# A Fourier-mixing and two-FFN kernel on one core: its arithmetic on GpSimd moved to VectorE and ScalarE

## The chip, the core and the metric

The kernel runs on one core of a Trainium2 chip. The engines are named as the profile names them: PE is TensorE (PEld its weight loads), DVE is VectorE, ACT is ScalarE, POOL is GpSimd, SP is the engine that only issues DMAs. Each engine runs its own instructions in the order in which they stand in the program and waits for the others by semaphores. The metric is the time of one execution on the device in microseconds (us), as the median of several runs.

## The reference

```python
X = np.fft.rfft(x, axis=1)                      # x: 4 x 3072 x 256
Yr = Xr @ w_r - Xi @ w_i + b_r
Yi = Xr @ w_i + Xi @ w_r + b_i
Y  = shrink(Yr, 0.01) + 1j * shrink(Yi, 0.01)   # sign(v) * max(|v| - 0.01, 0)
y  = np.fft.irfft(Y, n=3072, axis=1)
xk = mu_k * y + (1 - mu_k) * y_prev             # y_prev: one position earlier
xr = mu_r * y + (1 - mu_r) * y_prev
k  = np.maximum(xk @ w_k, 0.0)                  # w_k: 256 x 1024
v  = k * k @ w_v                                # w_v: 1024 x 256
x  = sigmoid(xr @ w_rr) * v
h  = x @ w_in                                   # w_in: 256 x 2048
g  = h * np.clip(h + 3, 0, 6) / 6
out = g @ w_out                                 # w_out: 2048 x 256
```

[...]

## The kernel before

Every matmul is done in three passes on a high and a low part of each operand (`three`: high by high, low by high, high by low). So each operand is split first: ACT copies it rounded to its high part, and a subtraction (source minus high part) gives the low part. `split` (lines 145 to 148) does this and is told which engine subtracts, DVE or POOL.

The program has two halves. The first half, up to about 1062 us, does the Fourier mixing of four batches and the first FFN; the second half does the second FFN and has no arithmetic on POOL.

For each batch the mixing has three parts. `s1` reads chunks of x (tiles `a`, split into `ah` and `al`) and writes a first transform through DRAM. `mid` runs over 12 blocks j: `s2` (a transform into PSUM, split into `Xh` and `Xl`), `mix` (24 matmuls with w_r and w_i, then the shrink on DVE: `yf`, `ym`, `yf`), and `ia` (the first part of the inverse, from `yh` and `yl`, with the table tile `tt`, three buffers, loaded from DRAM by DMAs on POOL's queue). `ib` reads chunks again (`a`, `ah`, `al`) and ends on DVE with `ysb`, which frees its PSUM tile. A block of `mid` is 42 matmuls.

The first FFN works on 24 tiles of 512 tokens. `prep` makes a tile's two inputs (`xf` on ACT and DVE, then `kh` on ACT and `kl`); `u_r` and four units `u_k` with their `u_v` follow, 12 matmuls each for `pr`, `pk` and `acc`, so 108 for a tile. After each `pk` ACT makes `g` and its square `gh`, DVE multiplies `g` by itself (L549) and subtracts (`gl`, L550), and `acc` uses them two units later. From the second batch on, the mixing of the next batch is interleaved with FFN units.

`Weights.decode` (lines 184 to 209) turns 512 columns of a 64-bit weight into high and low parts, in four steps between which other work of the program is recorded: (1) three operations on DVE on the exponent word (extract, clamp, subtract and scale: L195, L196, L197), (2) three more on DVE (sign and exponent L199, mantissa L200, sum L201), (3) a product on POOL (L203), (4) `split` with its subtraction on POOL. There are 25 such jobs: 9 while the first batch is mixed, 16 (w_in, w_out) between about 800 and 1062 us, while the last tiles of the first FFN run.

On POOL in the first half stand: the subtraction of every second chunk (`al`, 88 of 176 together with 24 of 48 in `mid`), of every second `yl` (24 of 48), one half of every `kl` (48, the other half on DVE), of every decoded or plain weight (27), of one `xl`, the 25 products of the decode, and the DMAs of the tables.

The names are those of the profile: `al<-a,ah` is the instruction that writes a tile `al` from `a` and `ah`.

Of the kernel before, what the change touches and what calls it, by code (L numbers as in the profile page):

```python
# [9 lines left out]
F32 = mybir.dt.float32  # L10
# [4 lines left out]
ALU = mybir.AluOpType  # L15
# [88 lines left out]
def fourier_mix_ffn_kernel(  # L104
# [37 lines left out]
    def ptile(name):  # L142
        return ps.tile([128, 1024], F32, tag="h", name=name)

    def split(src, h, l, eng):

        nc.scalar.activation(h, src, AF.Copy)  # L147
        eng.tensor_sub(l, src, h.bitcast(F32))  # L148

    def three(o, pairs, first=True, last=True, **kw):  # L150

# [7 lines left out]
    class Weights:  # L159
# [24 lines left out]
        def decode(self, staged, k, q, c, m):  # L184
            w, t = staged
            yield
            hi, lo = self.hi[:, k : k + q, c : c + m], self.lo[:, k : k + q, c : c + m]
            if self.wide:
                w = w.rearrange("p k (n s) -> p k n s", s=2)
                low, high = w[:, :, :, 0], w[:, :, :, 1]  # L190
                a = t[:, 0].rearrange("p (k n) -> p k n", k=q)
                f = t[:, 1].rearrange("p (k n) -> p k n", k=q)
                ai, au = a.bitcast(I32), a.bitcast(U32)
                ts, stt = nc.vector.tensor_scalar, nc.vector.scalar_tensor_tensor
                ts(au, high, 20, 0x7FF, op0=ALU.logical_shift_right, op1=ALU.bitwise_and)  # L195
                ts(ai, ai, 916, 1170, op0=ALU.max, op1=ALU.min)  # L196
                ts(ai, ai, 916.0, 2.0**23, op0=ALU.subtract, op1=ALU.mult)  # L197
                yield
                stt(au, high, 0x80000000, au, op0=ALU.bitwise_and, op1=ALU.bitwise_or)  # L199
                ts(high, high, 0xFFFFF, 0x100000, op0=ALU.bitwise_and, op1=ALU.bitwise_or)  # L200
                stt(f, low, 2.0**-32, high, op0=ALU.mult, op1=ALU.add)  # L201
                yield
                nc.gpsimd.tensor_mul(f, f, a)  # L203
            else:
                f = w
                yield
                yield
            yield
            split(f, hi, lo, nc.gpsimd)

    def decoder(jobs, stage):

# [14 lines left out]
    with tc.manual_schedule(engines=order):  # L227
# [6 lines left out]
        mus = cst.tile([128, 2, 2], F32, name="mus")  # L234
        omu = cst.tile([128, 2, 2], F32, name="omu")
        half = cst.tile([128, 1], F32, name="half")
        bias = fp.tile([128, 3, D], F32, name="bias")
        tex = fp.tile([128, 2, 64], F32R, name="tex")

# [17 lines left out]
        def split_chunks(upto):  # L257
            while head["split"] < min(upto, head["load"]):
                n = head["split"]
                a, p = live[n]  # L260
                h = fp.tile([128, 2, D], F32R, tag="ah", bufs=4, name="ah")
                l = fp.tile([128, 2, D], F32R, tag="al", bufs=4, name="al")
                split(a, h[:p], l[:p], nc.gpsimd if n % 2 else nc.vector)
                live[n] = (h[:p], l[:p])
                head["split"] += 1

# [44 lines left out]
        def mid(b):  # L311
# [6 lines left out]
            def s2(j):  # L318
                ((h, l),) = take(1)
                t = tt[b, j]  # L320
                p = ptile("s2")
                for g in range(2):
                    for dt in range(2):
                        d = slice(128 * dt, 128 * dt + 128)
                        hl = (h[:, g, d], l[:, g, d])
                        if j or g:
                            c = 512 * g + 192 * dt
                            three(p[:, c : c + 192], [(hl, (t[:, g, 0:192], t[:, g, 192:384]))])
                        else:
                            c = 256 * dt  # L330
                            three(p[:, c : c + 64], [(hl, (t[:, g, 0:64], t[:, g, 192:256]))])
                            three(p[:, c + 64 : c + 128], [(hl, (tex[:, 0], tex[:, 1]))])
                            three(p[:, c + 128 : c + 256], [(hl, (t[:, g, 64:192], t[:, g, 256:384]))])
                xh = fp.tile([128, 896], F32R, tag="Xh", bufs=2, name="Xh")
                xl = fp.tile([128, 896], F32R, tag="Xl", bufs=2, name="Xl")
                if j == 0:
                    split(p[:, 0:896], xh, xl, nc.vector)
                else:
                    two = lambda v: v.rearrange("p (g f) -> p g f", g=2)
                    split(two(p)[:, :, 0:384], two(xh[:, 0:768]), two(xl[:, 0:768]), nc.vector)  # L340
                xx[j] = (xh, xl)

            def mix(j):
# [19 lines left out]

            def split_y(j):
                y, *yy[j] = yy[j]
                split(y, *yy[j], nc.gpsimd if j % 2 else nc.vector)

            def ia(j):
                yh, yl = yy.pop(j)
# [94 lines left out]
        load_chunks(5)  # L464
        nc.vector.memset(zero, 0.0)
        nc.vector.memset(half, 0.5)

        def vectors():
            for i, v in enumerate((b_r, b_i)):
# [18 lines left out]
        def prep(i):  # L488

            if i:  # L490
                y = yt.pop(i)
                before, now = [(0, TOK, y)], [(0, TOK, y[:, :, N1:])]
            else:

                y1, y2 = ysb.pop(1), ysb.pop(2)
                before = [(0, 352, y1[:, :, 32:]), (352, TOK, y2)]
                now = [(0, 256, y1[:, :, 128:]), (256, TOK, y2)]
            for w in (1, 0):
                xf = kb.tile([128, 2, TOK], F32, tag="xf", bufs=1, name="xf")
                for a in range(2):  # L500
                    for lo, hi, y in before:
                        nc.scalar.activation(xf[:, a, lo:hi], y[:, a, 0 : hi - lo], AF.Copy, scale=omu[:, w, a : a + 1])
                yield
                for a in range(2):
                    for lo, hi, y in now:
                        o = xf[:, a, lo:hi]
                        nc.vector.scalar_tensor_tensor(  # L507
                            o, y[:, a, 0 : hi - lo], mus[:, w, a : a + 1], o, op0=ALU.mult, op1=ALU.add
                        )
                yield  # L510
                h = kb.tile([128, 2, TOK], F32R, tag="kh", bufs=3, name="kh")
                l = kb.tile([128, 2, TOK], F32R, tag="kl", bufs=3, name="kl")
                nc.scalar.activation(h, xf, AF.Copy)  # L513
                nc.gpsimd.tensor_sub(l[:, 0], xf[:, 0], h[:, 0].bitcast(F32))  # L514
                nc.vector.tensor_sub(l[:, 1], xf[:, 1], h[:, 1].bitcast(F32))  # L515
                xs[i, w] = h, l
                yield

# [65 lines left out]
        def split_2(i):  # L584
            h = kb.tile([128, 2, TOK], F32R, tag="kh", bufs=3, name="xh2")
            l = kb.tile([128, 2, TOK], F32R, tag="kl", bufs=3, name="xl2")
            split(xt[i], h, l, nc.gpsimd)
            xt[i] = (h, l)

        def u_i(i, j):  # L590
# [10 lines left out]
            l = kb.tile([128, 1024], F32R, tag="gl", bufs=3, name="gl2")  # L601
            nc.scalar.activation(g, p, AF.Relu, bias=half, scale=1.0 / 6.0)
            nc.vector.scalar_tensor_tensor(g, g, 1.0, p, op0=ALU.min, op1=ALU.mult)
            split(g, h, l, nc.vector)
            hg[i, j] = (h, l)


# [375 lines left out]
```

## Time and profile before

| | |
|---|---|
| median of 3 runs | 2106.92 us (2104.93 to 2109.38) |
| the profiled execution's own time | 2105.2 us |
| span of its trace | 2103.4 us |
| PE busy, share of the span | 2017.2 us, 96% |
| DVE busy | 1579.2 us, 75% |
| ACT busy | 1290.6 us, 61% |
| POOL busy | 363.9 us, 17% |

Busy time is the time in which an engine worked on an instruction; an instruction that is held up in its middle counts as busy all the while. PE's matmuls are pipelined and overlap in the records, so a busy PE need not be at its peak; the number of matmuls in a stretch tells more. The granted clock (PEclk) is 1.00 where PE had 2.4 GHz throughout a stretch and 0.50 where it had 1.2 GHz.

### The profile page before, as it was taken

How to read it: one execution, taken by the hardware profiler on the slowest of the kernel's cores; microseconds unless marked ns; L12 is line 12 of the kernel's file. 1: busy time of each engine (PE TensorE's matmuls, PEld its weight loads, DVE VectorE, ACT ScalarE, POOL GpSimd, SP SyncE). 2: the span in 40 equal slices, each digit the busy share in tenths (PEclk: the TensorE clock that was granted, in tenths of full speed). 3: DMA queues.
4: the chain of work that ended last, by engine and by line, in shares of the span. 5: the costliest groups of instructions: out<-in, count | busy, mean ns of one | idle time of the engine just before them, and what ended most of it. 6: DMA issues, size and time to landing. Idle time of an engine off the chain costs nothing.

```text
span 2103.4 us, 34043 instructions
## 1 busy us (share of the span) xinstructions
PE 2017.2 (96%) x13928; PEld 1870.1 (89%) x13928; DVE 1579.2 (75%) x1858; ACT 1290.6 (61%) x1867; POOL 363.9 (17%) x276
## 2 busy tenths in 40 slices
PE   6878999999899999989998999999999999999999
PEld 4867997899789988768788999999999999999999
DVE  2988667667666677989978778777777777777775
ACT  5456447555664465545546677767776777667765
POOL 4455223222332132333310000000000000000000
PEclk7978999999999999999999999999999999999999
DMA  8765446543663242212101010100010011001100
GB/s 268 232 190 169 126 117 197 183 118 113 198 189 115 83 157 93 83 64 91 56 21 31 21 31 21 31 21 28 24 31 21 23 30 31 21 21 31 31 11 21
DMA packets 106991, 175.88 MB, mean 84 GB/s; under 512 B 12945, under 2 KB 63314, under 8 KB 106834
## 3 DMA queue, kind: packets, MB, share of 16 engines
q1 hardware_dynamic: 96034, 141.76, 21.8%
q0 software_dynamic: 10480, 31.67, 5.5%
q8 instruction: 109, 1.79, 0.4%
q14 instruction: 48, 0.39, 0.1%
q10 hardware_dynamic: 320, 0.26, 0.0%
HBM read 110.35 MB, written 63.31 MB: 83 GB/s over the span
## 4 chain that ended last, share of the span: by engine, by line
PE 79%; DVE 12%; ACT 3%; issue 2%; DMA 2%; POOL 1%; SPq 0%; ACTq 0%; DVEq 0%
PE oacc L773 25%; PE rq L773 15%; PE acc L156 9%; PE pk L156 7%; PE cc L773 6%; PE mix L156 5%; PE s L156 4%; PE pr L156 2%; DVE g L549 2%; DVE xf L507 2%; DVE gl L550 1%; PE ia L156 1%; PE ib L419 1%; PE ib L418 1%; DVE kl L515 1%
## 5 line engine op out<-in xcount | busy, mean ns | idle before, releaser
L773 PE MATMUL oacc<-wo_hi,gl 128*128 128x256 f32 x1536 | 432.9, 282 | 0.3 <-DVE gl L747 0.3
L773 PE MATMUL oacc<-wo_hi,gh 128*128 128x256 f32 x1536 | 432.0, 281 | 0.0
L773 PE MATMUL oacc<-wo_lo,gh 128*128 128x256 f32 x1536 | 429.9, 280 | 0.0
L773 PEld LDWEIGHTS oacc<-wo_hi,gh 128*128 128x128 f32 x1536 | 290.1, 189 | 0.2
L773 PEld LDWEIGHTS oacc<-wo_hi,gl 128*128 128x128 f32 x1536 | 289.3, 188 | 0.7 <-DVE gl L747 0.5
L773 PEld LDWEIGHTS oacc<-wo_lo,gh 128*128 128x128 f32 x1536 | 289.8, 189 | 0.0
L729 DVE TENSOR_TENSOR c<-rq,s 128x512 f32<-128x512 f32 x184 | 127.2, 691 | 184.8 <-ACT s L725 184.8
L742 DVE SCALAR_TENSOR_TENSOR g<-g,c 128x1024 f32<-128x1024 f32 x184 | 225.4, 1225 | 42.7 <-ACT g L741 37.9
L773 PE MATMUL rq<-th,sw 128*128 128x256 f32 x1104 | 221.0, 282 | 7.3 <-issue 7.3
L747 DVE TENSOR_TENSOR gl<-g,gh 128x1024 fp32r<-128x1024 f32 x184 | 223.6, 1215 | 1.2 <-ACT gh L746 1.2
L746 ACT ACTIVATE gh<-g 128x1024 fp32r<-128x1024 f32 x184 | 195.3, 1061 | 45.0 <-DVE g L742 45.0
L741 ACT ACTIVATE g<-c,half 128x1024 f32<-128x1024 f32 x184 | 210.7, 1145 | 2.2 <-DVE c L730 1.4
L709 ACT ACTIVATE s<-rq 128x512 f32<-128x512 f32 x184 | 110.2, 599 | 131.2 <-PE rq L773 129.0
L544 ACT ACTIVATE g<-pk 128x1024 f32<-128x1024 f32 x96 | 97.8, 1019 | 150.8 <-PE pk L156 150.6
L773 PEld LDWEIGHTS rq<-th,sw 128*128 128x128 f32 x1104 | 169.6, 189 | 7.4 <-issue 7.4
L156 PE MATMUL acc<-gl,wv_hi 128*128 128x512 f32 x384 | 152.8, 398 | 7.9 <-DVE gl L550 7.9
L148 POOL TENSOR_TENSOR al<-a,ah 96x512 fp32r<-96x512 f32 (+1 forms) x88 | 124.1, 1410 | 209.2 <-ACT ah L147 199.6
L773 PE MATMUL rq<-tl,sw 128*128 128x256 f32 x552 | 154.5, 280 | 2.7 <-DVE tl L676 2.7
L156 PE MATMUL pk<-kh,wk_hi 128*128 128x512 f32 x384 | 152.1, 396 | 2.8 <-ACT kh L513 2.5
L156 PE MATMUL acc<-gh,wv_hi 128*128 128x512 f32 x384 | 152.5, 397 | 0.0
L156 PE MATMUL pk<-kl,wk_hi 128*128 128x512 f32 x384 | 151.4, 394 | 1.2 <-POOL kl L514 1.2
L156 PE MATMUL acc<-gh,wv_lo 128*128 128x512 f32 x384 | 151.2, 394 | 0.0
(151 smaller groups left out, 5291.7 us busy)
## 6 DMA issues: line engine op xcount, KB each, us to landing
tt<-in_tab_dram POOLq DMA_DIRECT2D x40, 640.0 KB, 5.0
yt<-sc_y SPq DMA_DIRECT2D x23, 608.0 KB, 4.0
a<-in_x_dram SPq DMA_DIRECT2D x64, 192.0 KB, 3.3
sc_a<-s1sb SPq DMA_DIRECT2D x32, 384.0 KB, 3.7
a<-sc_a SPq DMA_DIRECT2D x48, 256.0 KB, 3.4
sc_b<-iasb SPq DMA_DIRECT2D x48, 256.0 KB, 4.9
a<-sc_b SPq DMA_DIRECT2D x64, 192.0 KB, 2.8
sc_y<-ysb SPq DMA_DIRECT2D x32, 384.0 KB, 2.8
```

The source lines that it names most:

```text
L148: eng.tensor_sub(l, src, h.bitcast(F32))
L156: nc.tensor.matmul(o, a, c, start=first and i == 0, stop=last and i == n - 1, **kw)
L507: nc.vector.scalar_tensor_tensor(o, y[:, a, 0 : hi - lo], mus[:, w, a : a + 1], o, op0=ALU.mult, op1=ALU.add)
L544: nc.scalar.activation(g, p, AF.Relu)
L549: nc.vector.tensor_mul(g, g, g)
L709: nc.scalar.activation(s[:, 1:3].rearrange("p a n -> p (a n)"), rq, AF.Copy)
L729: nc.vector.tensor_add(c[:, 1::2], two(rq), s[:, 0:2])
L741: nc.scalar.activation(g, c, AF.Relu, bias=half, scale=1.0 / 6.0)
L742: nc.vector.scalar_tensor_tensor(g, g, 1.0, c, op0=ALU.min, op1=ALU.mult)
L746: lambda: nc.scalar.activation(h, g, AF.Copy),
L747: lambda: nc.vector.tensor_sub(l, g, h.bitcast(F32)),
L773: return lambda: nc.tensor.matmul(o, lhs, rhs, start=start, stop=stop, skip_group_check=True)
```

## The change

All of POOL's arithmetic goes elsewhere. `split` loses its engine argument and always subtracts on DVE; `kl` is one subtraction of twice the width on DVE; the decode's product is on DVE. In the decode's first step the clamp and the scaling (two operations on DVE) become two ACT operations with Relu: the first gives max(1170 - a, 0), the second max(254 - that, 0) times 2 to the 23rd, which is the same clamp to 916..1170 less 916. They take their constants from a new tile `top`, set by two small memsets. POOL keeps the DMAs of the tables.

```diff
-    def split(src, h, l, eng):
+    def split(src, h, l):
         nc.scalar.activation(h, src, AF.Copy)
-        eng.tensor_sub(l, src, h.bitcast(F32))
+        nc.vector.tensor_sub(l, src, h.bitcast(F32))
...
                 ts(au, high, 20, 0x7FF, op0=ALU.logical_shift_right, op1=ALU.bitwise_and)
-                ts(ai, ai, 916, 1170, op0=ALU.max, op1=ALU.min)
-                ts(ai, ai, 916.0, 2.0**23, op0=ALU.subtract, op1=ALU.mult)
+                nc.scalar.activation(f, ai, AF.Relu, bias=top[:, 0], scale=-1.0)
+                nc.scalar.activation(ai, f, AF.Relu, bias=top[:, 1], scale=-(2.0**23))
                 yield
                 stt(au, high, 0x80000000, au, op0=ALU.bitwise_and, op1=ALU.bitwise_or)
...
-                nc.gpsimd.tensor_mul(f, f, a)
+                nc.vector.tensor_mul(f, f, a)
...
-            split(f, hi, lo, nc.gpsimd)
+            split(f, hi, lo)
...
-                split(a, h[:p], l[:p], nc.gpsimd if n % 2 else nc.vector)
+                split(a, h[:p], l[:p])
...
-                split(y, *yy[j], nc.gpsimd if j % 2 else nc.vector)
+                split(y, *yy[j])
...
+        nc.vector.memset(top[:, 0], 1170.0)
+        nc.vector.memset(top[:, 1], 254 * 2.0**23)
...
-                nc.gpsimd.tensor_sub(l[:, 0], xf[:, 0], h[:, 0].bitcast(F32))
-                nc.vector.tensor_sub(l[:, 1], xf[:, 1], h[:, 1].bitcast(F32))
+                nc.vector.tensor_sub(l, xf, h.bitcast(F32))
...
-            split(xt[i], h, l, nc.gpsimd)
+            split(xt[i], h, l)
```

PE's instructions stand in the same order before and after. Three places where other engines' rows change:

DVE in `mid` of the first batch, one pair of blocks with one decode job, before (`Xl`, `yl`, `yf`, `ym` are the block's own work, `stt` and `stw` the decode's):

```order
L148 TENSOR_TENSOR Xl<-s_643,Xh 128x768
L148 TENSOR_TENSOR yl<-yf,yh 128x512
L195 TENSOR_SCALAR stt<-stw 128x512
L196 TENSOR_SCALAR stt<-stt 128x512
L197 TENSOR_SCALAR stt<-stt 128x512
L359 TENSOR_TENSOR yf<-mix,bias 128x512
L360 TENSOR_SCALAR ym<-yf 128x512
L361 SCALAR_TENSOR_TENSOR yf<-yf,ym 128x512
L148 TENSOR_TENSOR al<-a,ah 128x512
L148 TENSOR_TENSOR Xl<-s_719,Xh 128x768
L199 SCALAR_TENSOR_TENSOR stt<-stw,stt 128x512
L200 TENSOR_SCALAR stw<-stw 128x512
```

The same place of the changed program (line numbers are three higher, since lines were added):

```order
L148 TENSOR_TENSOR Xl<-s_646,Xh 128x768
L148 TENSOR_TENSOR yl<-yf,yh 128x512
L204 TENSOR_TENSOR stt<-stt 128x512
L196 TENSOR_SCALAR stt<-stw 128x512
L361 TENSOR_TENSOR yf<-mix,bias 128x512
L362 TENSOR_SCALAR ym<-yf 128x512
L363 SCALAR_TENSOR_TENSOR yf<-yf,ym 128x512
L148 TENSOR_TENSOR al<-a,ah 128x512
L148 TENSOR_TENSOR Xl<-s_722,Xh 128x768
L148 TENSOR_TENSOR yl<-yf,yh 128x512
L148 TENSOR_TENSOR wk_lo<-stt,wk_hi 128x512
L200 SCALAR_TENSOR_TENSOR stt<-stw,stt 128x512
```

The clamp and the scaling have left DVE; a product (L204), a `yl` and a weight's low part have come, and the `al` of every block instead of every second one. On ACT the two Relu operations stand behind the block's `Xh` and ahead of the next `ah`.

DVE in an `ib` stretch of the second batch, between FFN units, before:

```order
L423 TENSOR_TENSOR ysb<-ib,co 128x2x192 x2
L148 TENSOR_TENSOR al<-a,ah 96x512
L507 SCALAR_TENSOR_TENSOR xf<-yt,mus,xf 128x512 x2
L549 TENSOR_TENSOR g<-g 128x1024
L550 TENSOR_TENSOR gl<-g,gh 128x1024
L423 TENSOR_TENSOR ysb<-ib,co 128x2x192 x2
L148 TENSOR_TENSOR al<-a,ah 96x512
L515 TENSOR_TENSOR kl<-xf,kh 128x512
```

The same place of the changed program:

```order
L425 TENSOR_TENSOR ysb<-ib,co 128x2x192 x2
L148 TENSOR_TENSOR al<-a,ah 96x512 x2
L511 SCALAR_TENSOR_TENSOR xf<-yt,mus,xf 128x512 x2
L552 TENSOR_TENSOR g<-g 128x1024
L553 TENSOR_TENSOR gl<-g,gh 128x1024
L425 TENSOR_TENSOR ysb<-ib,co 128x2x192 x2
L148 TENSOR_TENSOR al<-a,ah 96x512 x2
L518 TENSOR_TENSOR kl<-xf,kh 128x1024
```

Each pair of chunks now has both of its `al` on DVE, and `kl` has twice its width; the order is otherwise the same.

POOL from the start of the program, before (`f` and `tex` are small tables, `tt` the tables of `mid`):

```order
L463 DMA f_93<-in_small_dram 96x192
L148 ISA
L148 TENSOR_TENSOR al<-a,ah 96x512 x9
L293 DMA tex<-in_ext_dram 128x128
L308 DMA tt<-in_tab_dram 128x2x384
L148 TENSOR_TENSOR al<-a,ah 96x512
L308 DMA tt<-in_tab_dram 128x2x384
```

And now:

```order
L465 DMA f_93<-in_small_dram 96x192
L295 DMA tex<-in_ext_dram 128x128
L310 DMA tt<-in_tab_dram 128x2x384 x2
L310 DMA tt<-in_tab_dram 128x1280 x6
```

Only DMAs are left in POOL's queue, so nothing but a free buffer holds them.

## Rows read from the trace of the kernel before

**Rows 1.** Stretches: busy us (instructions) of PE, PEld, DVE, ACT, POOL; PEclk, DMA, GB/s.

```profile
53.00:125.00 72.00, 61.31 (x452) 58.56 (x452) 66.83 (x86) 28.72 (x47) 36.47 (x32) 0.93 0.69 205
125.00:190.00 65.00, 49.88 (x198) 40.56 (x198) 50.71 (x60) 40.60 (x70) 33.85 (x23) 0.66 0.60 184
...
330.00:400.00 70.00, 63.06 (x312) 52.05 (x310) 51.60 (x53) 46.52 (x71) 25.03 (x19) 0.93 0.62 188
...
800.00:840.00 40.00, 40.00 (x178) 33.11 (x178) 29.42 (x35) 21.07 (x24) 8.83 (x5) 1.00 0.20 68
840.00:960.00 120.00, 110.26 (x469) 88.13 (x468) 107.81 (x115) 64.84 (x75) 42.88 (x24) 0.99 0.24 79
960.00:1062.00 102.00, 100.14 (x439) 81.78 (x438) 98.01 (x102) 55.21 (x63) 40.86 (x24) 1.00 0.20 64
1062.00:2103.00 1041.00, 1026.62 (x8581) 1020.97 (x8579) 789.04 (x953) 706.60 (x1057) 0.57 (x1) 0.99 0.09 25
```

**Rows 2.** Waits of PE in the first half: us in total, times, longest.

```profile
PE ib L418 <- DVE ysb L423: 18.6, 5, 5.7
...
PE ia L156 <- ACT yh L147: 9.7, 5, 2.3
PE acc L156 <- DVE gl L550: 7.9, 9, 1.9
...
PE s L156 <- DMA tt<-in_tab_dram: 3.5, 2, 3.3
```

**Rows 3.** Instructions in order of time, 339 to 346 us, all engines.

```profile
339.93 1.95 POOL L148 TENSOR_TENSOR al<-a,ah 96x512 fp32r<-96x512 f32 x1 [1.55 <-ACT ah L147]
...
340.76 3.46 DVE L550 TENSOR_TENSOR gl<-g,gh 128x1024 fp32r<-128x1024 f32 x1
...
341.85 1.29 POOL L514 TENSOR_TENSOR kl<-xf,kh 128x512 fp32r<-128x512 f32 x1
...
345.94 0.47 PE L156 MATMUL s<-al,f 96*96 96x512 f32 x1 [2.31 <-DVE al L148]
```

**Rows 4.** Costliest groups on the page: a DVE subtraction of the second half.

```profile
L747 DVE TENSOR_TENSOR gl<-g,gh 128x1024 fp32r<-128x1024 f32 x184 | 223.6, 1215 | 1.2 <-ACT gh L746 1.2
```

**Rows 5.** Instructions in order of time, 53 to 56 us: DVE, then POOL's next.

```profile
53.66 0.68 DVE L199 SCALAR_TENSOR_TENSOR stt<-stw,stt 128x512 uint32<-128x512 uint32 x1
...
54.38 0.43 DVE L200 TENSOR_SCALAR stw<-stw 128x512 uint32<-128x512 uint32 x1
...
55.63 1.27 POOL L203 TENSOR_TENSOR stt<-stt 128x512 f32<-128x512 f32 x1 [4.97 <-DVE stt L201]
```

**Rows 6.** DVE's groups by shape in the first half, 0 to 1062 us.

```profile
L549 DVE TENSOR_TENSOR g<-g 128x1024 f32<-128x1024 f32 x96 | 135.5, 1411 | 8.9 <-ACT gh L548 8.5
L550 DVE TENSOR_TENSOR gl<-g,gh 128x1024 fp32r<-128x1024 f32 x95 | 134.2, 1412 | 4.2
L507 DVE SCALAR_TENSOR_TENSOR xf<-yt,mus,xf 128x512 f32<-128x512 f32 x92 | 78.9, 898 | 0.0
L515 DVE TENSOR_TENSOR kl<-xf,kh 128x512 fp32r<-128x512 f32 x48 | 56.2, 1171 | 9.8 <-ACT kh L513 9.8
L148 DVE TENSOR_TENSOR al<-a,ah 96x512 fp32r<-96x512 f32 x64 | 51.5, 805 | 48.9 <-ACT ah L147 48.9
```

**Rows 7.** DVE's groups in the first batch's mid, 53 to 125 us: the decode's.

```profile
L201 DVE SCALAR_TENSOR_TENSOR stt<-stw 128x512 f32<-128x512 uint32 x6 | 9.0, 1502 | 0.2
...
L199 DVE SCALAR_TENSOR_TENSOR stt<-stw,stt 128x512 uint32<-128x512 uint32 x6 | 7.9, 1310 | 0.0
...
L200 DVE TENSOR_SCALAR stw<-stw 128x512 uint32<-128x512 uint32 x6 | 7.4, 1228 | 0.3
```

**Rows 8.** POOL's largest group, whole span.

```profile
L148 POOL TENSOR_TENSOR al<-a,ah 96x512 fp32r<-96x512 f32 (+1 forms) x88 | 124.1, 1410 | 209.2 <-ACT ah L147 199.6 <-PE s L156 5.0 <-issue 4.3
```

**Rows 9.** ACT's operation with one per-partition constant, first half by shape.

```profile
L502 ACT ACTIVATE xf<-yt,omu 128x512 f32<-128x512 f32 x92 | 61.3, 715 | 29.4 <-DVE kl L515 18.6 <-POOL kl L514 10.7
```

**Rows 10.** DVE's longest waits in the first half, us in total, times, longest.

```profile
DVE Xl L148 <- ACT Xh L147: 60.4, 31, 4.7
```

More of the change, by code (lines that the diff above doesn't have):

```diff
@@ L236, in fourier_mix_ffn_kernel @@
         half = cst.tile([128, 1], F32, name="half")
+        top = cst.tile([128, 2, 1], F32, name="top")
         bias = fp.tile([128, 3, D], F32, name="bias")
@@ L336, in s2 @@
                 if j == 0:
-                    split(p[:, 0:896], xh, xl, nc.vector)
+                    split(p[:, 0:896], xh, xl)
                 else:
                     two = lambda v: v.rearrange("p (g f) -> p g f", g=2)
-                    split(two(p)[:, :, 0:384], two(xh[:, 0:768]), two(xl[:, 0:768]), nc.vector)
+                    split(two(p)[:, :, 0:384], two(xh[:, 0:768]), two(xl[:, 0:768]))
                 xx[j] = (xh, xl)
@@ L603, in u_i @@
             nc.vector.scalar_tensor_tensor(g, g, 1.0, p, op0=ALU.min, op1=ALU.mult)
-            split(g, h, l, nc.vector)
+            split(g, h, l)
             hg[i, j] = (h, l)
```

## The prediction

> **What bounds the kernel now.** I first read the stretches [rows 1], because POOL's arithmetic all lies in the first 1062 us: behind that POOL is busy for 0.57 us, so the second half can't change. In the first half I look for stretches in which PE is short of work, since PE's own program stays as it is, and only such time can be got back or added to. From 800 to 840 us PE runs FFN units at full speed: 178 matmuls in 40 us, 4.45 per us. From 840 to 960 us it gets 469, where 4.45 x 120 would be 534, so 14.6 us are lost; from 960 to 1062 us 439, so 3.3 us more. DVE is busy 107.8 of those 120 us. From 53 to 125 us, `mid` of the first batch, DVE is busy 66.8 of 72 us and PE only 61.3 us at a mean clock of 0.93. From 330 to 400 us, an `ib` stretch between FFN units, PE stands idle for 6.9 us, and the clock falls to 0.93: it was at 1.2 GHz for (1 - 0.93)/0.5 = 14% of 70 us, or 9.8 us, half of which, 4.9, is lost. That pattern comes three times, once for each later batch.
>
> Then the waits of PE [rows 2]: the longest go back to DVE (`ysb` 18.6 us in five waits, `gl` 7.9 us in nine), and `yh`, on ACT, itself waits for the shrink on DVE. So DVE is what PE waits for.
>
> Why is DVE late? A `gl` begins at 340.76 us and takes 3.46 us, with two POOL subtractions beside it [rows 3], and PE then waits 2.31 us for the `al` that stands behind it on DVE. The same subtraction takes 1.215 us in the second half, where POOL does nothing [rows 4], and a mean of 1.41 in the first [rows 6]. In five microseconds in which POOL is idle, a decode's L199 takes 0.68 and its L200 0.43 [rows 5]; in the whole of `mid`, with POOL at work, 1.31 and 1.23 [rows 7]. So a DVE instruction is stretched when POOL works beside it, by the remainder of POOL's instruction. That is the cost which the change removes.
>
> **The change part by part.** I use these clean prices: 1.215 us for a subtraction of 1024 columns, 0.69 for one of 512 (0.68 measured, with a little for its start), 0.43 for a tensor_scalar.
>
> *DVE's work in the first half.* Added are 88 `al` [rows 8], 24 `yl`, 25 products, 27 low parts of weights and the wider `kl`: (88 + 24 + 25 + 27) x 0.69 = 113.2, 48 x (1.215 - 0.69) = 25.2, one `xl` 1.2, together 139.6 us. Removed are 50 tensor_scalars, at their clean price 21.5 us. The stretch that goes [rows 6]: 96 x 0.196 = 18.8, 95 x 0.197 = 18.7, 92 x 0.208 = 19.1 on `xf`, 48 x 0.481 = 23.1 on `kl`, 64 x 0.115 = 7.4: 87.1 us; and in `mid` of the first batch [rows 7] 6 x (0.81 + 0.62 + 0.80) = 13.4. Net: 139.6 - 21.5 - 87.1 - 13.4 = +17.6 us, with the stretch of the other 19 decode jobs still to come off. DVE's load over the half stays about level. A gain must come from where the work falls and from the long stretches, so I go by stretch.
>
> *840 to 1062 us.* A tile is 108 matmuls, 24.3 us of PE at 4.45 per us. DVE's work for it becomes 8 subtractions or products of 1024 columns and two `kl`, 10 x 1.215 = 12.2, and four `xf` and two final products, 6 x 0.69 = 4.1; a decode job is 2 x 0.43 + 4 x 0.69 = 3.6 us, and with 16 jobs for 10 tiles that is 5.8. Sum 22.1 us, under PE's 24.3. DVE stops being the bound here, and of the 17.9 us lost I take **15** back (bounds 0 and 17.9).
>
> *The three `ib` stretches.* In each, DVE gets one more `al` for a pair of chunks (+0.69) ahead of the `ysb` that frees PE's PSUM tile, and loses the stretch: for the `gl` above 3.46 - 1.215 = 2.25. So a stall of this kind shrinks by about 1.6 us, by more where `xf` is stretched as well; it does not vanish. Of 6.9 + 4.9 = 11.8 us for one stretch I take 6; the repeat from 530 to 600 us holds the longest wait for `ysb`, 5.7 us, so 6 again, and 2 for the third: **14** (bounds -5, if all the stalls stay and each of seven pairs adds its 0.69, and 26).
>
> *`mid` of the first batch.* Removed 13.4 us of stretch and 5 jobs x 0.86 of clamps; added 6 `al`, 5 `yl`, 6 products and 5 low parts, 22 x 0.69 = 15.2. Net -2.5 us on a DVE that is busy 93% of the time. The waits for `yh` (9.7 us) come behind stretched decode instructions. I take **4** (bounds 2 and 10).
>
> *125 to 190 us.* PE is idle for 15 us here, at a clock of 0.66, for several reasons, transfers through DRAM among them. Two of the five waits for `ysb` are left for it: 18.6 less about 11.7 for the later ones is 6.9 us. I take **5** (bounds 0 and 6.9).
>
> *POOL's queue.* With only DMAs in it, the first three table tiles are loaded at the start and not behind the `al` of x's chunks. That saves PE's wait of 3.3 us for `tt` [rows 2]: **3**. Against it, 1.4 MB (two tiles of 384 columns and one of 640, 256 rows, 4 bytes) are moved while x is being read: at the 205 GB/s of the first stretch [rows 1] up to 7 us, if nothing of it fits into gaps (bounds -4 and 4).
>
> *ACT.* Fifty Relu operations with a per-partition constant, by the nearest row 0.715 us each [rows 9], 36 us in all. From 840 to 960 us ACT is busy 64.8 of 120 us, so it has the room; but ACT now waits in its order for DVE's first decode step. I take **-3** (bounds 0 and -36).
>
> ScalarE's row for such an operation, 0.715 us, is dearer than the 0.43 of the DVE operation that it replaces. The Trainium skill (ScalarE: Activation LUTs, Rules for kernel authors) says the same as a rule against this part of the change: relu, max and min belong on VectorE. By that rule the move costs 50 x (0.715 - 0.43) = 14 us of engine time; it lengthens the kernel only if ACT is what PE waits for, and the trace so far shows ACT 54% busy where most of the jobs lie.
>
> Sum: 15 + 14 + 4 + 5 + 3 - 3 = 38 us. The profiled execution took 2105.2 us (span 2103.4), which is 1.7 under the median of the runs shown, so 2105.2 - 38 = **2067 us**.
>
> **The rivals.**
> - *All the lost time comes back* (no stall in `ib`, the clock never falls): 17.9 + 26 + 10 + 6.9 + 4 = 65, or 2040 us. For it: the stalls shown are short chains. Against: in `ib` DVE gets as much new work as it loses. 0.14.
> - *Only the end comes back.* The stalls of `ib` and of the first 190 us have other last causes (ACT, transfers), and the new `al` and `kl` fill the gap: 15 + 3 = 18, or 2087 us. For it: DVE's sum stays level. 0.18.
> - *ACT becomes the holder.* By the rule above, which speaks for this one: the Relu pairs delay `g`, `co` and `Xh`, and all 36 us land on PE: 2105 - 38 + 36 = 2103, no change. It decides where ACT is nearly full, and it is not. 0.04.
> - *The other side: the decode's round trip.* DVE's second decode step (L199) now waits for two ACT operations that stand behind other work in ACT's queue, and `ysb`, `gl` and `al` are queued behind it. DVE's waits for ACT's `Xh` last 60.4/31 = 1.9 us each [rows 10]. There are 25 such trips; at 1.5 us each the 41 us of gain (ahead of ACT's -3) are nearly gone, at 2.5 the kernel is 22 us slower: 2127 us. Against it: a block or half a unit of other work lies between the two steps. 0.06.
> - *POOL was not what stretched DVE.* Then the stretch stays, and DVE has 139.6 - 21.5 = 118 us more; where DVE is the bound (some 300 of 1062 us) about 33 us land on PE: 2138 us. Rows 3 and 5 speak against it, and so does a rule: the Trainium skill (SBUF — State Buffer, Who interferes with whom) says that a VectorE instruction with two SBUF inputs and a GpSimd one that reads SBUF exclude each other; by it the trace's 3.46 us is one instruction held by two of POOL's. 0.03.
>
> **How the numbers follow.** My own case, 25 to 62 us of gain, has 0.55; with the rivals, faster than before by over 0.2% (4 us, about what a measurement of this kernel can tell) is 0.55 + 0.14 + 0.18 = 0.87, the same 0.04, slower 0.09. Leaving out the last three rivals and the outer ends of the first two, the range is 2043 to 2093 us; my own case alone runs from 2043 to 2080.
>
> **What would show it.** Right: `g`, `gl` at 1.21 us throughout the first half, `kl` at 1.21 with its double width, L199 at 0.68; from 840 us on 4.4 matmuls per us and DVE near 90% busy; the waits for `ysb` under half of 18.6 us and the clock at 1.00 in the `ib` stretches; no wait for `tt` before 60 us; the second half as long as before. Wrong: DVE waiting for the decode's Relu (more than 20 us in all), `ysb` waits as long as before behind the second `al`, or x's loads in the first 30 us later by some microseconds.

## The result, and the profile after

| | before | after |
|---|---|---|
| median of 4 runs each | 2106.14 us (2104.93 to 2109.38) | 2082.28 us (2080.50 to 2082.47) |
| ratio | | 0.9885 (95% interval 0.9873 to 0.9898) |
| span of the profiled execution | 2103.4 us | 2080.7 us |
| PE, DVE, ACT, POOL busy | 2017.2, 1579.2, 1290.6, 363.9 us | 1992.8, 1549.8, 1323.2, 35.0 us |

The kernel became 24 us faster where 38 were predicted. The total is in the range, but it is the sum of parts that are quite unlike those of the prediction.

VectorE's prices are the ones that the prediction took as clean, but for `xf`. The groups of DVE's instructions in the first 1055 us after the change (operation, out<-in, shape, count | busy us, mean ns | idle before it and its releaser):

```profile
L553 DVE TENSOR_TENSOR gl<-g,gh 128x1024 fp32r<-128x1024 f32 x96 | 117.6, 1225 | 4.0
L552 DVE TENSOR_TENSOR g<-g 128x1024 f32<-128x1024 f32 x96 | 117.1, 1220 | 32.6 <-ACT gh L551 32.6
L511 DVE SCALAR_TENSOR_TENSOR xf<-yt,mus,xf 128x512 f32<-128x512 f32 x92 | 64.7, 745 | 0.0
L518 DVE TENSOR_TENSOR kl<-xf,kh 128x1024 fp32r<-128x1024 f32 x48 | 58.5, 1220 | 16.0 <-ACT kh L517 16.0
L200 DVE SCALAR_TENSOR_TENSOR stt<-stw,stt 128x512 uint32<-128x512 uint32 x25 | 17.1, 685 | 0.0
L201 DVE TENSOR_SCALAR stw<-stw 128x512 uint32<-128x512 uint32 x25 | 10.7, 429 | 0.9
```

Against [rows 6], `g` and `gl` fell from 1411 and 1412 ns to 1220 and 1225, `xf` from 898 to 745, and `kl` takes 1220 ns for twice the columns that took 1171. For `xf` the prediction took 690. The first two operations of the decode's second step take 685 and 429 ns (L200 and L201 now) where `mid` had 1310 and 1228 (L199 and L200, [rows 7]). With POOL's arithmetic gone the stretch is gone, so POOL's work was what stretched them.

The stretches after the change (busy us and instructions of PE, PEld, DVE, ACT, POOL; PEclk, DMA, GB/s), to be held against [rows 1]:

```profile
53.00:125.00 72.00, 61.46 (x479) 57.43 (x478) 63.74 (x106) 38.18 (x63) 7.56 (x12) 1.00 0.73 220
330.00:400.00 70.00, 68.86 (x378) 58.44 (x377) 51.15 (x71) 49.95 (x76) 1.07 (x2) 0.98 0.68 210
840.00:960.00 120.00, 105.87 (x442) 83.05 (x441) 88.18 (x108) 69.04 (x84) 0.00 (x0) 0.97 0.23 75
960.00:1062.00 102.00, 95.93 (x411) 77.55 (x410) 78.79 (x96) 61.26 (x72) 0.00 (x0) 0.98 0.17 56
```

The `ib` stretch gains, as was forecast: 378 matmuls in place of 312 (the same 70 us of time, though not quite the same piece of the program), and the clock at 0.98. The stretch on which the largest term rested, the one of the last decode, does not. From 840 to 960 us DVE fell from 107.8 to 88.2 us, and PE did **fewer** matmuls than before, 442 for 469. Nobody is full there: something waits.

Some of the waits after the change (who waited for whom: total us, times, longest); left out at the top are waits of POOL's queue, waits of the second half and ACT's for PE:

```profile
...
ACT stt L197 <- DVE stt L196: 91.8, 25, 6.2
DVE g L552 <- ACT gh L551: 32.6, 20, 3.6
...
PE acc L156 <- DVE gl L553: 13.3, 14, 2.0
...
DVE omu L480 <- DMA mus<-in_moe_mu_r_dram: 10.6, 1, 10.6
...
PE ia L156 <- DVE yl L148: 8.6, 11, 2.0
...
PE ib L420 <- DVE ysb L425: 7.0, 5, 2.4
```

PE's wait for `ysb` fell from 18.6 to 7.0 us [rows 2]. The first of these lines is new: ACT's first Relu of every piece waits for DVE's first decode step, 91.8 us in 25 times, 53.3 us of it from 840 to 1062 us. One of these in order of time (ACT, DVE and the two waits of PE):

```profile
987.32 1.23 DVE L553 TENSOR_TENSOR gl<-g,gh 128x1024 fp32r<-128x1024 f32 x1
988.46 1.41 DVE L511 SCALAR_TENSOR_TENSOR xf<-yt,mus,xf 128x512 f32<-128x512 f32 x2
989.79 0.68 DVE L204 TENSOR_TENSOR stt<-stt 128x512 f32<-128x512 f32 x1
990.39 0.42 DVE L196 TENSOR_SCALAR stt<-stw 128x512 uint32<-128x512 uint32 x1
990.85 0.72 ACT L197 ACTIVATE stt<-stt,top 128x512 f32<-128x512 int32 x1 [5.33 <-DVE stt L196]
991.60 0.73 ACT L198 ACTIVATE stt<-stt,top 128x512 int32<-128x512 f32 x1
992.24 1.00 ACT L547 ACTIVATE g<-pk 128x1024 f32<-128x1024 f32 x1
993.14 1.04 ACT L517 ACTIVATE kh<-xf 128x1024 fp32r<-128x1024 f32 x1
994.09 1.04 ACT L551 ACTIVATE gh<-g 128x1024 fp32r<-128x1024 f32 x1
994.22 1.22 DVE L518 TENSOR_TENSOR kl<-xf,kh 128x1024 fp32r<-128x1024 f32 x1 [3.40 <-ACT kh L517]
995.18 0.50 PE L156 MATMUL acc<-gh,wv_hi 128*128 128x512 f32 x1 [1.26 <-ACT gh L551]
995.36 1.22 DVE L552 TENSOR_TENSOR g<-g 128x1024 f32<-128x1024 f32 x1
996.61 1.23 DVE L553 TENSOR_TENSOR gl<-g,gh 128x1024 fp32r<-128x1024 f32 x1
...
997.89 0.50 PE L156 MATMUL acc<-gl,wv_hi 128*128 128x512 f32 x1 [1.98 <-DVE gl L553]
```

ACT stands still for 5.33 us at the Relu, from 985.52 us on, while DVE works off `g` (ahead of the first line shown), `gl`, two `xf` and a product before it comes to L196. Behind the Relu in ACT's queue stand `g`, `kh` and `gh`. They are late now; so DVE, just released from its own load, idles 3.40 us for `kh`; then PE waits 1.26 us for `gh` and 1.98 us for `gl`. The two engines hold each other in turn.

For the rest of the document a table of places in the program, each the start of an instruction in ACT's timeline: `r` of the FFN1 tiles 3, 13, 15 and 22 (counted from 0; tile 3 lies behind the mixing of the first batch and ahead of the later batches' `ib` stretches, tile 13 in the last of these, tile 15 behind it; from tile 15 to the second FFN runs the last decode), the first `g` of the second FFN, and the span. Times in us; the kernels e1 to e12 follow below.

| kernel | tile 3 | tile 13 | tile 15 | tile 22 | second FFN | span | second FFN to end |
|---|---|---|---|---|---|---|---|
| before | 304.3 | 764.7 | 824.7 | 1011.0 | 1062.1 | 2103.4 | 1041.3 |
| after | 300.3 | 742.8 | 803.6 | 1009.9 | 1055.2 | 2080.7 | 1025.5 |
| e1 | 303.9 | 763.9 | 823.8 | 1009.9 | 1061.0 | 2087.8 | 1026.8 |
| e3 | 294.5 | 735.4 | 796.2 | 970.0 | 1019.0 | 2044.6 | 1025.6 |
| e4 | 308.8 | 768.9 | 829.0 | 1052.5 | 1100.2 | 2150.3 | 1050.1 |
| e5 | 288.4 | 729.2 | 790.0 | 969.0 | 1018.6 | 2043.4 | 1024.8 |
| e12 | 289.1 | 728.4 | 789.2 | 963.0 | 1012.0 | 2037.3 | 1025.3 |

From before to after, 21.9 us are gained by tile 13, only 1.1 are left at tile 22, 6.9 at the second FFN; and another 15.8 come in the second half, where the prediction said that nothing can change.

### The profile page after: what moved, and what is told of

Read it like the earlier page. It is cut to its first block, busy times and chain, and to the rows that moved or that the text cites. A ratio compares the mean times of both kernels' runs of the same rounds, so it can differ in the third digit from the quotient of the medians.

```text
span 2080.7 us, 33798 instructions
## 1 busy us (share of the span) xinstructions
PE 1992.8 (96%) x13928; PEld 1844.5 (89%) x13928; DVE 1549.8 (74%) x1975; ACT 1323.2 (64%) x1917; POOL 35.0 (2%) x63
## 4 chain that ended last, share of the span: by engine, by line
PE 76%; DVE 14%; ACT 6%; issue 2%; DMA 2%; SPq 0%; ACTq 0%; DVEq 0%
PE oacc L776 24%; PE rq L776 15%; PE acc L156 8%; PE pk L156 7%; PE cc L776 6%; PE mix L156 5%; PE s L156 4%; DVE g L552 2%; DVE gl L553 2%; PE pr L156 2%; DVE xf L511 1%; PE ia L156 1%; DVE kl L518 1%; PE ib L421 1%; PE ib L420 1%
## 5 line engine op out<-in xcount | busy, mean ns | idle before, releaser
L776 PE MATMUL oacc<-wo_hi,gl 128*128 128x256 f32 x1536 | 426.7, 278 | 0.6 <-DVE gl L750 0.6
L776 PE MATMUL oacc<-wo_hi,gh 128*128 128x256 f32 x1536 | 427.1, 278 | 0.0
L776 PE MATMUL oacc<-wo_lo,gh 128*128 128x256 f32 x1536 | 425.4, 277 | 0.0
L148 DVE TENSOR_TENSOR al<-a,ah 96x512 fp32r<-96x512 f32 (+1 forms) x176 | 114.9, 684 | 55.2 <-ACT ah L147 55.2
```

Of the source, the lines that this page charges most:

```text
L148: nc.vector.tensor_sub(l, src, h.bitcast(F32))
L776: return lambda: nc.tensor.matmul(o, lhs, rhs, start=start, stop=stop, skip_group_check=True)
```

## Experiments

Two questions: what gave back the gain in the decode stretch, and what made the second half faster. Each run was timed beside the kernel before, to which its ratio refers; the medians of that kernel were 2104.2 to 2106.1 us, so two or three us between kernels that were timed apart say nothing.

The kernel's tiles lie in SBUF, of which the program fills a left and a right side. In its allocation the tiles of the left side lie 32 bytes further after the change, since `top` takes 32 bytes there: `gh` starts at 18176 before and at 18208 after, `sw` at 109056 and 109088. The right side's `wi` and `wo` stay. In the kernel before, the left tiles behind that place start at multiples of 64 bytes and `wi`, `wo` 32 bytes past one; after it all of them lie 32 bytes past one.

**e1: the place alone.**

```diff
         half = cst.tile([128, 1], F32, name="half")
+        pad = cst.tile([128, 2, 1], F32, name="pad")
...
         nc.vector.memset(half, 0.5)
+        nc.vector.memset(pad, 0.0)
```

> The kernel before, with one unused constant of 8 bytes per partition put behind `half`, which shifts every tile behind it on the left side of SBUF by 32 bytes, as the change's new constant `top` does; no operation moves. Theory P (the place): the second half of the program runs at another pace because its tiles lie elsewhere. Then the stretch from 1200 to 1300 us holds 864 matmuls in place of 850, as after the change, the second half is 15 us shorter, and the whole is 2089 to 2092 us. Rival S (the state in which the engines enter the second half sets its pace): the place does nothing, 850 matmuls, 2104 to 2108 us. Rival N (a difference between two executions): the same as S.

Measured: 2089.27 us against 2105.01, ratio 0.9921 (0.9906 to 0.9935). The stretch from 1200 to 1300 us (us, PE busy and its matmuls, PEclk, DMA share, GB/s), of the kernel before, of the changed one and of e1:

```profile
1200.00:1300.00 100.00, 100.00 (x850) 1.00 0.08 23
```

```profile
1200.00:1300.00 100.00, 100.00 (x864) 1.00 0.10 28
```

```profile
1200.00:1300.00 100.00, 100.00 (x864) 1.00 0.10 27
```

PE is never idle in any of the three and has 2.4 GHz throughout, yet 864 matmuls fit where 850 did: 115.7 ns from one to the next in place of 117.6. No operation was moved; one small memset was added at the start. The second half is 14.5 us shorter, the first 1.1. Theory P stands; S and N fall.

**e2: the changed kernel, with the place of before modulo 64 bytes.**

```diff
-        top = cst.tile([128, 2, 1], F32, name="top")
+        top = cst.tile([128, 2, 8], F32, name="top")
...
```

> The changed kernel with `top` made 64 bytes per partition, so that the tiles behind it lie a whole 64 bytes further than in the kernel before. Theory P, if what counts is the place modulo 64 bytes: the second half goes back to 850 matmuls in 100 us and the time to 2096 to 2099 us. Theory P, if any shift will do, or rival S: 864 matmuls and 2081 to 2083 us.

Measured: 2104.06 us, ratio to the kernel before 0.9994 (0.9984 to 1.0003).

```profile
1200.00:1300.00 100.00, 100.00 (x849) 1.00 0.10 28
```

The old pace is back, and with it nearly the old time, 5 us above what was expected. In its profile the second FFN begins at 1054.4 us, 7.7 before that of the kernel before, and the second half takes 1044.2 us, 2.9 more. So of the 24 us the shift by 32 bytes, which the change brings only in passing, makes 15.7 (e1) to 21.8 (the changed kernel against e2), and all the moved **operations** together between 1 and 8, as losses and gains among them nearly cancel (e3 parts them).

**e3: the clamps back on VectorE.**

```diff
-                nc.scalar.activation(f, ai, AF.Relu, bias=top[:, 0], scale=-1.0)
-                nc.scalar.activation(ai, f, AF.Relu, bias=top[:, 1], scale=-(2.0**23))
+                ts(ai, ai, 916, 1170, op0=ALU.max, op1=ALU.min)
+                ts(ai, ai, 916.0, 2.0**23, op0=ALU.subtract, op1=ALU.mult)
```

> The changed kernel, with the decode's clamps put back from two relus on ScalarE to the two VectorE operations they were (the constant `top` stays, so that no tile moves). Theory A (ScalarE's relus, which stand at the head of its queue until VectorE has done the decode's first step, are what gave back the gain between 840 and 1062 us): ScalarE's wait of 91.8 us for that step is gone, the stretch from the 16th FFN1 tile to the first tile of the second FFN is 10 to 18 us shorter than in the changed kernel, and the whole is 2063 to 2073 us. Rival V (VectorE has no room for the 0.85 us per piece in the decode stretch, so that it becomes the bound again): 2080 to 2095 us, with VectorE at more than 95 of 120 us between 840 and 960 us. Rival 0 (the wait is covered): 2080 to 2084 us.

Measured: 2046.66 us, ratio to the kernel before 0.9723 (0.9708 to 0.9737), by the medians 35.6 us below the changed kernel (34 by the ratios, 0.9885 - 0.9723 of 2105): about twice the most that was expected. The stretches 840 to 960 and 960 to 1019 us of e3 (columns as in the stretches above):

```profile
840.00:960.00 120.00, 118.23 (x520) 97.15 (x519) 110.31 (x147) 68.88 (x79) 0.00 (x0) 1.00 0.27 88
960.00:1019.00 59.00, 59.00 (x262) 48.83 (x261) 53.70 (x67) 32.94 (x39) 0.00 (x0) 1.00 0.17 56
```

PE does 520 matmuls in 120 us where the changed kernel did 442, and DVE is busy for 110.3 us with it. Rival V took that for a sign that VectorE binds again; it was above 95 us, and PE nevertheless lost only 1.8 us. A VectorE that is 92% busy with clean instructions keeps up; before, 107.8 us of stretched ones were not enough.

**e4: the kernel before, with only the clamps moved to ScalarE** (the arithmetic on GpSimd stays; `top` has 64 bytes).

```diff
-                ts(ai, ai, 916, 1170, op0=ALU.max, op1=ALU.min)
-                ts(ai, ai, 916.0, 2.0**23, op0=ALU.subtract, op1=ALU.mult)
+                nc.scalar.activation(f, ai, AF.Relu, bias=top[:, 0, 0:1], scale=-1.0)
+                nc.scalar.activation(ai, f, AF.Relu, bias=top[:, 1, 0:1], scale=-(2.0**23))
...
```

> The kernel before, with only the decode's clamps changed to two relus on ScalarE (all arithmetic on GpSimd stays; the constant is 64 bytes per partition, so that the tiles keep their place modulo 64 bytes). Theory A: ScalarE waits some 90 us for the decode's first step, the decode stretch from 840 to 1062 us grows by 8 to 18 us, and the whole is 2112 to 2124 us. Rival V (VectorE is what binds that stretch in the kernel before, so that 0.85 us less per piece helps): 2090 to 2102 us.

Measured: 2149.23 us, ratio 1.0200 (1.0183 to 1.0217). The sign is theory A's, the size (44 us) more than twice its own. 38.1 us of it lie ahead of the second FFN (1100.2 against 1062.1), nearly the 36.2 that the same operations cost on the changed kernel (1055.2 against 1019.0): what the relus cost hardly depends on where the rest of the arithmetic is. The other 8.8 us came in the second half, which did 844 matmuls in 100 us; its tiles lie as in the kernel before modulo 64 bytes, and all of them at the very addresses of e2, which did 849. So this is not explained.

**e5: the relus one step of the decoder later.** The decoder gets one step more for it.

```diff
                 ts(au, high, 20, 0x7FF, op0=ALU.logical_shift_right, op1=ALU.bitwise_and)
+                yield
                 nc.scalar.activation(f, ai, AF.Relu, bias=top[:, 0], scale=-1.0)
...
```

> The changed kernel, with the two relus on ScalarE recorded one step of the decoder later than VectorE's extraction of the exponent (and all that follows in the decode one step later too). Theory A (what costs is that ScalarE meets the relus before VectorE has come to the step they need): ScalarE's wait of 91.8 us falls under 20 us and the whole comes to 2046 to 2060 us, near the kernel with the clamps on VectorE (2046.7 us). Rival B (two more passes on ScalarE cost by themselves, 25 times 1.44 us): ScalarE's wait goes, but the time stays within 2068 to 2084 us.

Measured: 2045.33 us, ratio 0.9718 (0.9703 to 0.9732). The same 50 relus on ScalarE, and 37 us less. What is left of the wait (total us, times, longest):

```profile
ACT stt L198 <- DVE stt L196: 10.9, 6, 4.5
```

**e6: the work of the relus without their wait.** On top of e3:

```diff
+                nc.scalar.activation(f, high.bitcast(I32), AF.Relu, bias=top[:, 0], scale=-1.0)
+                nc.scalar.activation(f, high.bitcast(I32), AF.Relu, bias=top[:, 0], scale=-1.0)
                 ts(au, high, 20, 0x7FF, op0=ALU.logical_shift_right, op1=ALU.bitwise_and)
```

> The kernel with the clamps on VectorE, and beside them, for each piece, two passes of ScalarE of the relus' size that read the loaded words as they came, so that they wait for nothing of VectorE (they write where the decode writes later, and change no result). This is the work of the relus without their wait. Theory A: 2046 to 2054 us. Rival B: 2068 to 2084 us.

Measured: 2050.26 us, ratio 0.9737 (0.9721 to 0.9753): 3.6 us more than e3 (2.9 by the ratios), about the size of the intervals (0.15% of 2105 is 3.2 us). The two passes in its profile are 38 us of ScalarE's work, and it was idle ahead of them for less than 1 us:

```profile
L197 ACT ACTIVATE stt<-stw,top 128x512 f32<-128x512 int32 x25 | 19.2, 769 | 0.8
L196 ACT ACTIVATE stt<-stw,top 128x512 f32<-128x512 int32 x25 | 18.8, 752 | 0.1
```

**e7: the wait without the work.** On top of e3, behind the clamps:

```diff
                 ts(ai, ai, 916.0, 2.0**23, op0=ALU.subtract, op1=ALU.mult)
+                nc.scalar.activation(top[:, 0, 1:2], t[:, 0, 0:1], AF.Copy)
...
```

> The kernel with the clamps on VectorE, and behind them, for each piece, one pass of ScalarE over a single column of VectorE's result: the wait of the relus without their work (one result column, read by nobody). Theory A: ScalarE waits 80 us or more for VectorE's clamp, and the whole takes 2072 to 2100 us. Rival B: 2046 to 2054 us.

Measured: 2076.73 us, ratio 0.9868 (0.9853 to 0.9882): 30.1 us more than e3, for 25 copies of one column. Its wait and its stretch from 840 to 960 us:

```profile
ACT top L199 <- DVE stt L198: 114.4, 25, 7.0
```

```profile
840.00:960.00 120.00, 108.87 (x454) 86.22 (x455) 96.15 (x125) 61.00 (x78) 0.00 (x0) 0.97 0.22 69
```

454 matmuls, near the changed kernel's 442. Theory A stands and B falls: the cost is the place in ScalarE's queue, not the passes.

**e8: `omu` later.** On top of e3, the operation goes out of `vectors()` and stands ahead of `fs = stream(later)`:

```diff
-            nc.vector.tensor_scalar(omu, mus, -1.0, 1.0, op0=ALU.mult, op1=ALU.add)
...
+        nc.vector.tensor_scalar(omu, mus, -1.0, 1.0, op0=ALU.mult, op1=ALU.add)
         fs = stream(later)
```

> The kernel with the clamps on VectorE, and the one small operation that makes `omu` out of `mus` moved from step 7 of the first stretch to where that stretch ends. Theory M (at the start, four subtractions of the first batch's `mid` stand on VectorE behind that operation, which waits 10.3 us for `mus`; before the change half of them stood on GpSimd's queue): the first `Xh` begins 2 to 4 us sooner, and the time is 2 to 4 us shorter, 2043 to 2045 us. Rival T (the tables, which are now loaded from the first microseconds on, delay `a` itself): no difference, 2046 to 2048 us.

Measured: 2045.94 us, ratio 0.9723 (0.9709 to 0.9737), against 0.9723 of e3. The first `Xh` in ACT's timeline, of e3 and of e8:

```profile
50.26 0.92 ACT L147 ACTIVATE Xh<-s 128x896 fp32r<-128x896 f32 x1 [4.95 <-PE s L156]
```

```profile
47.98 0.92 ACT L147 ACTIVATE Xh<-s 128x896 fp32r<-128x896 f32 x1 [2.83 <-PE s L156]
```

It does begin 2.3 us sooner, so the mechanism is right, but `r` of tile 0 starts at 163.7 us in both: what lies between takes the gain up. It isn't on the path.

**e9 and e10: where the right side lies.** On top of e3, a pool of 32 bytes ahead of the right side's first one; e10 also makes `top` 64 bytes.

```diff
+        rp = ctx.enter_context(tc.tile_pool(name="rp", bufs=1, side="right"))
+        pad = rp.tile([128, 2, 1], F32, name="pad")
         fp = ff.enter_context(tc.tile_pool(name="fp", bufs=1, side="right"))
...
```

> The kernel with the clamps on VectorE, with an unused constant of 8 bytes at the far end of the right side of SBUF as well, which moves all tiles of that side (of the second half's: `wi`, `wo`) by 32 bytes: the tiles of the left side stay 32 bytes past a multiple of 64, those of the right side now lie on one. Theory R (what counts is that the tiles of both sides have the same place modulo 64 bytes): 850 matmuls or fewer from 1200 to 1300 us and 2060 to 2066 us. Theory L (what counts is where the left side's tiles lie, 32 bytes past a multiple of 64 is the good place): 864 matmuls, 2045 to 2049 us.

> As the run before, with `top` made 64 bytes, so that the tiles of both sides lie on multiples of 64 bytes. Theory R: 864 matmuls or more from 1200 to 1300 us, 2040 to 2049 us. Theory L: 850 matmuls, 2060 to 2066 us.

Measured: 2067.75 us (ratio 0.9819, 0.9803 to 0.9834) and 2070.04 us (0.9829, 0.9814 to 0.9844), with 844 and 845 matmuls from 1200 to 1300 us. The same line as for e1, of e4, e9 and e10:

```profile
1200.00:1300.00 100.00, 100.00 (x844) 1.00 0.09 24
```

```profile
1200.00:1300.00 100.00, 100.00 (x844) 1.00 0.08 22
```

```profile
1200.00:1300.00 100.00, 100.00 (x845) 1.00 0.08 22
```

By the pace, theory R was right on e9 and wrong on e10, theory L the other way round, so both fall; the times lie 2 to 4 us above the ranges even where the pace was right. What the runs show is a table: 864 or 865 matmuls in 100 us only where both sides lie 32 bytes past a multiple of 64 (the changed kernel, e1, e3); 844 to 850 in the three other combinations (left and right: 0 and 32 in the kernel before, e2 and e4; 32 and 0 in e9; 0 and 0 in e10).

The two are of use in another way: they are the changed kernel without the relus and without the good place. Their second FFN begins at 1021.2 and 1020.9 us, 41 us before that of the kernel before, and the whole is 36 to 38 us faster.

**e11: the first tables held back.** On top of e3, one column copied by GpSimd when the last tile of the first stage is there, ahead of the tables in its queue:

```diff
+                        nc.gpsimd.tensor_copy(top[:N1, 0, 1:2], flat(sb[:N1])[:, 0:1])
                         nc.gpsimd.dma_start(out=tex, in_=ext)
...
```

> The kernel with the clamps on VectorE, with one copy of a single column on GpSimd ahead of the first tables' loads, which waits for the last tile of the first batch's first stage: the tables of the first batch are loaded some 25 us later, about where the kernel before loaded them. Theory T (the early tables slow x's and `a`'s loads, and the work done at 53 us then lies behind): the first `Xh` starts 2 to 4 us sooner than 50.3 us, and the whole is 2 to 4 us shorter, 2043 to 2045 us. Rival C (the tables held back arrive later than `s2` wants them, as in the kernel before, where PE waited 3.5 us for them): first `Xh` 0 to 3 us later or the same, 2046 to 2050 us.

Measured: 2046.82 us, ratio 0.9719 (0.9703 to 0.9735). The first `Xh` starts at 49.2 us, 1.1 sooner than in e3, and the end is the same within the interval. The time lies in rival C's range, the sooner `Xh` fits neither expectation: theory T wanted 2 us at least.

**e12: the relus a step later in the first decode, the clamps on VectorE in the last.** Made of e3 and e5: with `late` true for `wr`, `wk`, `wv` (the edit is shown against the changed kernel).

```diff
...
-                nc.scalar.activation(f, ai, AF.Relu, bias=top[:, 0], scale=-1.0)
-                nc.scalar.activation(ai, f, AF.Relu, bias=top[:, 1], scale=-(2.0**23))
+                if self.late:
+                    yield
+                    nc.scalar.activation(f, ai, AF.Relu, bias=top[:, 0], scale=-1.0)
+                    nc.scalar.activation(ai, f, AF.Relu, bias=top[:, 1], scale=-(2.0**23))
+                else:
+                    ts(ai, ai, 916, 1170, op0=ALU.max, op1=ALU.min)
+                    ts(ai, ai, 916.0, 2.0**23, op0=ALU.subtract, op1=ALU.mult)
...
```

> The clamps as relus a step later where the first three weights are decoded (53 to some 250 us, where ScalarE has room and VectorE is 95% busy), and as VectorE's two operations where the last two are decoded (from some 790 us on). Theory K (the 6 us that the relus a step later gained by the 15th FFN1 tile, 790.0 against 796.2 us, are kept, since the clamps on VectorE bind nothing in the last decode): 2039 to 2042 us. Rival E (TensorE has no idle time left from 800 us on in the kernel with the clamps on VectorE, but something else, the loads of the decoded weights, sets the end of that stretch): 2045 to 2048 us.

Measured: 2038.01 us, ratio 0.9677 (0.9662 to 0.9691). The fastest of all, 44 us below the changed kernel. It keeps the 7 us that it is ahead of e3 at tile 15 up to the second FFN (1012.0 against 1019.0), as theory K said. (VectorE's 95% in that expectation holds from 53 to 125 us of e3; from 53 to 250 us it is 84%.)

## Why the prediction was right and wrong

The range held (2082 in 2043 to 2093) and the sign was right, but the prediction's own case was a gain of 38 us by the arithmetic, and e1 and e2 leave between 1 and 8 us of gain to it. Two errors, of 33 us one way (the relus) and of 16 the other (the second half), cancelled in part. That the total fell into the range is so far luck.

- **The step that failed: "I take -3 (bounds 0 and -36)" for ACT.** It measured 35.6 us (e3 against the changed kernel), at the bound that I gave and didn't choose. The same paragraph says that "ACT now waits in its order for DVE's first decode step", and then prices the room that ACT has. Room was not the question. e6 and e7 part the two: the passes cost 3.6 us, hardly clear of the noise, the wait 30.1.
- **The rival came close and looked at the wrong leg.** "The decode's round trip" had DVE wait for the Relu at L199 of before (L200 after). DVE never waited there; the step between gave ACT time enough. The other leg, ACT waiting for DVE, has no step between: both are recorded in one. My sign for it, "DVE waiting for the decode's Relu", could not have shown it. ACT's wait did what that rival said of DVE's: everything queued behind it came late.
- **The rule against the change.** The Trainium skill (ScalarE: Activation LUTs, Rules for kernel authors) wants relu, max and min on VectorE. Its advice agrees with e3. Its reason, time per element, is not what cost here: an operation took 0.72 us on ACT and 0.43 on DVE, but of the engine's work e6 found 3.6 us in the kernel's time. With the relus a step later (e5) they stay on ScalarE and cost nothing that was measured against e3 (0.9718 for 0.9723).
- **"840 to 1062 us: 15"**, without the relus, was right: in e3 the lead grows from 28.5 us at tile 15 to 43.1 at the second FFN, by 14.6. With them it shrank from 21.1 to 6.9.
- **"The three `ib` stretches: 14"** measured 18.7 in e3 (a lead of 9.8 us at tile 3, 28.5 at tile 15, with all that lies between) and 17.1 in the changed kernel. The first stretch gave the most: by tile 5, which starts at 399.9 us before and at 379.1 in e3, the lead has grown by 11.0 us, where 6 were taken.
- **`mid` 4, 125 to 190 us 5, the tables 3**: together 12, measured 9.8 in e3 by tile 3. The tables' own 3 did not come: PE's wait for `tt` went, but in the changed kernel the first `Xh` began 4.4 us later than before (48.8 against 44.5), with DVE held 10.6 us by `mus` (7.0 before) ahead of the subtractions that POOL used to share. e8 (without that wait) and e11 (the tables loaded later) show that neither matters in the end.
- **POOL stretched DVE**: right, by the groups of DVE shown above. The Trainium skill (SBUF — State Buffer, Who interferes with whom) says that a VectorE instruction with two SBUF inputs contends with a GpSimd one that reads SBUF; the trace agrees, with `gl` at 1412 ns beside POOL and 1225 without. The decode's L200, which reads one tile only, was stretched as well (1228 ns in `mid`, 429 without POOL's arithmetic). In the prediction's count of DVE's work `xf` was mis-sized: clean it takes 745 ns, not 690, so of the 19.1 us of stretch counted on it 14.1 were there.
- **"The second half can't change"**: wrong, by 15.8 us. It argued from the operations alone. The change also adds a constant, the constant moves the tiles, and e1 shows that this alone shortens the half by 14.5 us.

Without the relus and the shift the prediction's sum would have been 41 us. e3's first half gained 43.1, of which the shift may hold 1.1 (e1), which leaves 42; the first halves of e9 and e10, which have not that place, gained 41. So the sum for the moved arithmetic was right to 1 or 2 us, its three parts to less than 5: they measured 9.8, 18.7 and 14.6 in e3 where 12, 14 and 15 were taken.

What stays open: why the place counts. The runs show that it does, in both directions and with nothing else changed (e1, e2), and that both sides have a part in it (e9, e10). They do not show which tile it is, nor whether 64 bytes are the right measure; and 844, 849 and 850 matmuls in three kernels whose tiles lie alike modulo 64 bytes (e4, e2, before), two of them at the same addresses throughout (e4, e2), say that the place isn't all. What takes up the time that e8 gains at the start was not tried.

## What to carry to other kernels

An operation moved to another engine's queue is priced by what it waits for, and by who stands behind it, before it is priced by its length: if its input is made in the same step by a busier engine, put a step between the two, or leave it where its input is made. When a change adds even a small tile, tiles move, so run the old kernel with the same shift before the difference is put down to the operations. And a time inside the range proves little: here it took kernels with parts of the change to see that one part lost 36 us, another won 42, and the shift of the tiles won some 16.

## What the hardware showed unexpectedly

TensorE, never idle and at 2.4 GHz, took 115.7 or 117.6 ns from one matmul of 256 columns to the next (864 and 850 in 100 us) by a shift of SBUF tiles of 32 bytes; the extremes over all kernels were 844 and 865. One copy of a single column on ScalarE for each of 25 pieces cost 30 us, because it waited for VectorE (114.4 us in all) at the head of ScalarE's queue.
